# Another order for the first 300 calls of an attention and two-layer kernel on one core

## The chip, the cores and the metric

The kernel runs on one core of one Trainium2 chip. The metric is the device time of one execution in microseconds (us). The core has five engines that run side by side, each through its own list of instructions in order: TensorE (PE in the profile, its weight loads PEld), VectorE (DVE), ScalarE (ACT), GpSimd (POOL) and SyncE (SP), which here only issues transfers. Engines wait for each other by semaphores. Transfers (DMAs) are issued by SP, POOL and, at the end, ACT.

## The reference

Inputs are q, k, v of shape 8 x 12 x 448 x 64 (batch, heads, rows, width), two gains g_q, g_k of 64, and w_in (768 x 2048), w_out (2048 x 768), alpha (2048).

```
q_n = q / sqrt(mean(q*q) + 1e-6) * g_q          # each row of 64; k_n likewise
scores = (q_n @ k_n.T) / 8
attn = exp(scores - max) ; attn = attn / sum(attn)
x = (attn @ v), heads side by side              # 3584 x 768
h = x @ w_in                                    # 3584 x 2048
g = max(h, 0) + alpha * min(h, 0)
out = g @ w_out                                 # 3584 x 768
```

## The kernel before

The 96 heads are cut into 24 groups of four heads, numbered y = 0 to 23. Three groups make one batch b. A group goes through these steps, which the code calls by name with y as the first argument:

- `load_qk` brings q and k into `nat` (SP). There are four `nat` buffers of which a group takes two; the groups 2, 5 and 8 use `arena` instead, so that 5 has to wait until `scale` has read 2, and 4 until `scale` has read 1.
- `square`, `reduce`, `root`, `scale` are the norm: squares (POOL, L376, or ACT, L370), sums of a row (DVE, L395), 1/sqrt as Exp of Ln (ACT, L416 and L417), and the product in fp16 (L436; DVE for groups 1 to 3, POOL from 4 on).
- `turn` (or `turn_one`) transposes q and k by matmuls with an identity into PSUM and copies them out on DVE (L560 to L569, L513 to L523). The product of the two gains goes onto k in that copy.
- `score` (L588) is four small matmuls for one seventh of the keys, `soft` (L602) the exponential of it on ACT, 128x896 elements. A group has seven of each.
- `den` and `attend` (L613) are the sums and the products with v; `log` and `invert` (L666, L671) give the reciprocal of the sums on ACT, `times` (L709) writes the quotient into `xT` on DVE.

When the three groups of a batch are in `xT`, `up(b,ft)` (L726) makes one of 16 blocks of h; `slope` (L766 on ACT, L761 on DVE) writes alpha*h and `larger` (L772) the larger of the two. `begin(ft)` does the first four of six matmuls of `up(0,ft)` before group 2 is there; `up(0,2)` then also ends block 3. `down` and, later, four-product forms make the output.

Group 0 has a form of its own in smaller parts: `part_square`, `part_reduce`, `part_root`, `part_scale`, `part_turn`, `part_copy`. `spin(n)` are idle matmuls on zeros, in fp32 where no second argument is given (two records each) and in fp16 with `spin(n,0)`. `follow(y,nm)` is a POOL copy of one element of the scaled group: POOL waits there until that group is scaled. `gains()` multiplies g_q and g_k after `opening()` has loaded them and alpha into `rows` and has transposed `rows` (the tile `ct`, L1025).

All of it is written down as one list of calls, PLAN, and issued in this order under a manual schedule: each engine meets its instructions in the order of the list, and there is no planner behind it.

Scores have three places in PSUM: two tiles "sc", and one tile "acc", which a score takes with a last argument of 1. `den` and the pair of tiles for `begin(2)` and `begin(3)` take "acc" as well, `attend` takes "acc", "sc" or the two tiles "mm". The tiles "mm" (two) serve `turn`, `spin`, `up` and the other half of `attend`. A new user of a place waits until the last reader of the old one is done.

Of the kernel before, what the change touches and what calls it, by code (L numbers as in the profile page):

```python
# [48 lines left out]
soft(4,0) square(7,q) larger(0,8) up(0,11,0) load_qk(8) score(4,2,0) score(3,3,0) soft(3,5)
load_v(1) square(7,k) up(0,7,1) soft(4,1) slope(0,9) up(0,10,0) reduce(6,q) square(8,q) reduce(6,k)  # L50
load_w_out(2) soft(4,2) up(0,12,0) slope(0,11) larger(0,9) soft(3,3) score(3,4,0) slope(0,10)
score(4,3,0) larger(0,11) larger(0,10) slope(0,7) larger(0,7) up(0,13,0) soft(3,4) slope(0,12)
larger(0,12) turn(5) up(0,14,0) square(8,k) soft(4,3) score(4,6,0) slope(0,13) score(4,4,1) root(6)
slope(0,14) larger(0,13) up(0,15,0) scale(6,q) reduce(8,q) soft(4,4) score(5,4,0) larger(0,14)
scale(6,k) score(5,0,1) reduce(7,q) slope(0,15) larger(0,15) down(1,0,0) score(5,2,1) score(4,5,0)
soft(4,6) soft(5,0) soft(5,4) soft(5,2) score(5,1,0) soft(4,5) down(0,0,0) turn(6) load_w_out(3)
den(3+4,1) reduce(7,k) attend(3+4,0,0) score(5,5,0) score(5,6,0) soft(5,1) mix_weights(0,1) log(3+4)
invert(3+4) soft(5,5) soft(5,6) mix_weights(0,3) attend(3+4,1,0) score(6,0,1) score(5,3,0) soft(6,0)
score(6,4,0) down_end(0,0) down(2,0,0) soft(5,3) root(7) scale(7,q) load_qk(9) soft(6,4) scale(7,k)
den(5,0) attend(5,0,1) down_end(1,0) mix_weights(0,2) times(3+4,0,0) times(3+4,1,0) times(3+4,1,1)  # L60
load_qk(10) log(5) down(0,1,0) reduce(8,k) invert(5) down_end(2,0) times(5,0,1) times(5,0,0)
times(5,0,3) times(5,0,2) score(6,5,1) mix_weights(0,0) score(6,1,0) down_end(0,1) score(6,6,0)
soft(6,5) turn(7) up(1,1,1) square(9,q) down(1,1,0) root(8) reduce(9,q) soft(6,6) score(6,3,1)
score(7,0,0) slope(1,1) score(6,2,0) up(1,2,0) up(1,0,0) soft(6,1) soft(7,0) soft(6,3) square(9,k)
up(1,3,1) up(1,4,0) slope(1,2) slope(1,0) larger(1,1) down_end(1,1) reduce(9,k) root(9) larger(1,2)
# [1032 lines left out]
```

## Time and profile before

| | us |
|---|---|
| three runs | 410.44, 410.85, 411.13; median 410.85 |
| the profiled execution, its own time | 410.69 |
| its span, first to last instruction | 408.6 |
| PE, DVE, ACT, POOL busy | 395.3, 268.3, 270.4, 299.9 |
| first score | 14.24 |
| first `up(0,0)` | 41.30 |
| `attend(6+7,0,0)`, where both lists are the same again | 118.51 |

Times in the profile are counted from the first instruction. A line of the timeline gives start, length, engine, line, operation, tiles and count, and in brackets the idle time of the engine just before it and what ended that. A line with x6 is six instructions in a row whose length is from the start of the first to the end of the last; neighbours overlap a little, so that one exponential of 0.916 us follows the next after some 0.83 us. PE records overlap too: four matmuls of a score alone take 0.38 us from start to end, but two scores in a row 0.57.

### The profile page before, as it was taken

The numbers are of one execution on the slowest core, as the hardware profiler recorded it, in microseconds if no ns is written. First come the engines' busy times: TensorE is split into PE (matmuls) and PEld (weight loads), VectorE is DVE, ScalarE is ACT, GpSimd is POOL, SyncE is SP. The second block draws the span as 40 slices with busy tenths as digits, with TensorE's granted clock in tenths as the row PEclk, the third lists the DMA queues.
The fourth block names the chain that finished last, engine by engine and source line by source line (L and its number), as shares of the span: only waits on it lengthen the run. The fifth ranks groups of instructions, "written<-read, shape, count | busy, mean of one in ns | idle before, by whom it ended". The sixth has DMA issues, their size and how long they took to land.

```text
span 408.6 us, 11992 instructions
## 1 busy us (share of the span) xinstructions
PE 395.3 (97%) x5083; PEld 210.3 (51%) x5083; DVE 268.3 (66%) x480; ACT 270.4 (66%) x405; POOL 299.9 (73%) x200
## 2 busy tenths in 40 slices
PE   7688999999999999999999999999999999999996
PEld 3344445555455445554455455555555455655664
DVE  3957874676766685779678678886668545654422
ACT  5597686757885876767886987686876874245110
POOL 7977998497796998997796995589496809600780
PEclk9999999999999999999999999999999999999999
DMA  7999699796776794579952595794516000230143
GB/s 260 242 280 227 110 265 165 173 239 177 125 180 154 173 203 108 119 172 185 232 130 83 136 240 145 147 217 102 140 38 131 21 2 22 59 79 0 39 98 98
DMA packets 37222, 58.39 MB, mean 143 GB/s; under 512 B 4769, under 2 KB 28977, under 8 KB 37169
## 3 DMA queue, kind: packets, MB, share of 16 engines
q1 hardware_dynamic: 23232, 45.43, 43.2%
q0 software_dynamic: 13536, 11.81, 19.1%
q8 instruction: 39, 0.64, 0.7%
q10 hardware_dynamic: 400, 0.39, 0.3%
q14 instruction: 15, 0.11, 0.1%
HBM read 58.40 MB, written 11.01 MB: 170 GB/s over the span
## 4 chain that ended last, share of the span: by engine, by line
PE 88%; DVE 4%; DMA 3%; POOL 3%; issue 1%; POOLq 0%; DVEq 0%
PE hT L726 25%; PE hTa L726 9%; PE sc L588 8%; PE op L792 7%; PE qx L854 5%; PE av L613 5%; PE qz L854 4%; PE qc L854 4%; PE oq L854 4%; PE qxa L854 3%; PE avb L613 2%; PE dn L613 2%; PE oqm L854 2%; DMA w_in_sb<-in_moe_w_in_dram 2%; POOL nat L376 2%; DMA arena<-in_g_k_dram 2%
## 5 line engine op out<-in xcount | busy, mean ns | idle before, releaser
L602 ACT ACTIVATE expT<-sc 128x896 f16<-128x896 f32 x168 | 146.3, 916 | 40.9 <-PE sc L588 39.2
L726 PE MATMUL hT<-xT,w_in_sb 128*128 128x448 f16 x558 | 115.9, 353 | 1.6 <-DVE xT L709 1.4
L726 PEld LDWEIGHTS <-w_in_sb 128*128 128x128 f16 x768 | 73.0, 98 | 74.5 <-issue 9.9
L423 POOL TENSOR_TENSOR qs<-nat,rr 128x896 f16<-128x896 f32 x30 | 65.7, 2221 | 26.5 <-ACT rr L417 23.4
L766 ACT ACTIVATE gT<-hT,cols 128x448 f16<-128x448 f32 x92 | 58.4, 636 | 40.0 <-PE hT L726 38.9
L772 DVE TENSOR_TENSOR gT<-hT,gT 128x448 f16<-128x448 f32 x93 | 57.3, 619 | 38.2 <-ACT gT L766 37.5
L365 POOL TENSOR_TENSOR nat<-nat 128x896 f32<-128x896 f32 x30 | 50.7, 1697 | 8.1 <-DMA nat<-in_q_dram 7.7
L588 PE MATMUL sc<-qT,kT 64*32 64x448 f16 (+1 forms) x1092 | 49.4, 355 | 4.3 <-ACT expT L602 1.7
L854 PEld LDWEIGHTS <-gT 128*128 128x128 f16 x352 | 33.4, 98 | 25.5 <-issue 4.1
L726 PE MATMUL hTa<-xT,w_in_sb 128*128 128x448 f16 x198 | 42.9, 353 | 0.0
L842 POOL TENSOR_TENSOR gs<-gT 128x1024 f16<-128x1024 f16 x4 | 8.5, 2127 | 36.7 <-DVE gT L772 36.7
L709 DVE TENSOR_TENSOR xT<-av,rden 64x448 f16<-64x448 f32 (+1 forms) x37 | 27.2, 736 | 10.7 <-ACT rden L671 4.6
L386 DVE TENSOR_REDUCE sp<-nat 128x28 f32<-128x896 f32 x30 | 32.1, 1070 | 2.1 <-POOL nat L365 2.0
L588 PEld LDWEIGHTS <-kT 64*32 64x32 f16 (+1 forms) x1092 | 16.7, 93 | 32.4 <-issue 23.0
L792 PE MATMUL op<-w_out_sb,gT 128*128 128x384 f16 x176 | 30.3, 326 | 0.2 <-DVE xT L709 0.2
L766 ACT ACTIVATE gT<-hTa,cols 128x448 f16<-128x448 f32 x33 | 21.0, 636 | 10.5 <-PE hTa L726 10.0
L772 DVE TENSOR_TENSOR gT<-hTa,gT 128x448 f16<-128x448 f32 x33 | 20.4, 618 | 10.6 <-ACT gT L766 10.2
L613 PEld LDWEIGHTS <-vt 64*32 64x32 f16 x1344 | 19.7, 92 | 12.2 <-issue 1.9
L792 PEld LDWEIGHTS <-gT 128*128 128x128 f16 x192 | 18.3, 98 | 14.5 <-issue 3.0
L613 PE MATMUL av<-expT,vt 64*32 64x448 f16 x896 | 24.3, 350 | 0.0
L850 POOL TENSOR_TENSOR gT<-gT 128x1024 f16<-128x1024 f16 x11 | 23.5, 2133 | 0.0
L854 PEld LDWEIGHTS <-arena 128*128 128x128 f16 x136 | 12.6, 98 | 10.5 <-issue 2.3
(151 smaller groups left out, 572.5 us busy)
## 6 DMA issues: line engine op xcount, KB each, us to landing
nat<-in_q_dram SPq DMA_DIRECT2D x60, 216.0 KB, 4.1
nat<-in_k_dram SPq DMA_DIRECT2D x60, 216.0 KB, 5.0
out_dram<-osb SPq DMA_DIRECT2D x107, 96.0 KB, 3.1
vt<-in_v_dram POOLq DMA_DIRECT2D x8, 672.0 KB, 7.8
w_in_sb<-in_moe_w_in_dram POOLq DMA_DIRECT2D x24, 128.0 KB, 7.3
w_out_sb<-in_moe_w_out_dram POOLq DMA_DIRECT2D x4, 768.0 KB, 8.6
nat<-in_k_dram SPq DMA_DIRECT2D x6, 448.0 KB, 7.8
nat<-in_q_dram SPq DMA_DIRECT2D x5, 448.0 KB, 6.7
```

Of the source, the lines that this page charges most:

```text
L365: nc.gpsimd.tensor_mul(out=sqs[y, nm], in0=t[:, :, :HD], in1=t[:, :, :HD])
L386: nc.vector.tensor_reduce(out=parts[y][:, ts("qk".index(nm), 4 * J), :1], in_=sqs[y, nm], axis=AXIS_X, op=ALU.add,)
L423: nc.gpsimd.tensor_mul(out=t.rearrange("p j d n -> p n j d"), in0=nat[y, nm][:, :, :HD].rearrange("p (n j) d -> p n j d", j=J), in1=r.unsq ...
L588: nc.tensor.matmul(out=sc[ds(64 * g + m * c, m), par, :S].rearrange("p (j c) -> p j c", j=J), lhsT=kT[ds(64 * par, 64), j, g, ts(c, m)], r ...
L602: nc.scalar.activation(out=expT[y][:, j], in_=scs[y, j][:, :, :S], func=AF.Exp, scale=QK_SCALE, bias=EXP_BIAS,)
L613: nc.tensor.matmul(out=accs[g][ds(32 * n, 32), :S], lhsT=weights(g, y, par, c, j), rhs=expT[y][ds(64 * g, 64), j, par, :], start=(j == 0), ...
L709: nc.vector.tensor_mul(out=o, in0=p, in1=q)
L726: nc.tensor.matmul(out=hT[:, :S], lhsT=w_in_sb[:, block_of(g, i), ts(ft, 128)], rhs=xT[b][:, g, i, :], start=(i == 0 and g == 0), stop=(i ...
L766: nc.scalar.activation(out=g, in_=hT[:, :S], func=AF.Copy, scale=alpha_sb[:, ft : ft + 1])
L772: nc.vector.tensor_max(out=g, in0=hT[:, :S], in1=g)
L792: nc.tensor.matmul(out=op[:, :OH], lhsT=gT[:, ft, ts(tile % J, 128)], rhs=w_out_sb[:, ft, ts(oh, OH)], start=(ft == 0), stop=(ft == NF - 1),)
L854: nc.tensor.matmul(out=bank[:, c], lhsT=g[:, ft], rhs=v[:, ft, c], start=(first and ft == 0), stop=(ft == HF - 1), skip_group_check=True,)
```

## The change

The list of calls up to `fold(11)` is put in another order, and from there on it is the same. What changes with it:

- ScalarE takes the squares of 1k, 2q, 4q, 6q, 6k and 8k from GpSimd (1q was there already), and the copies out of PSUM of group 0's q and of a part of its k from VectorE. VectorE takes the slopes of blocks 6, 8, 9, 13, 14, 15 of batch 0 and 4 and 5 of batch 1; block 12 goes to ScalarE, 2 stays on VectorE and 3 goes to ScalarE.
- `rows` is filled by two gain transfers ahead of alpha, where it was alpha and four gain transfers. The transpose of `rows` is a call of its own, `factors()`, behind the transposes of q.
- v is loaded ahead of the first w_in piece; w_in comes in six pieces, 1 and 0 (rows below 512), 0 (rows above), 2 (above), 2 and 3 (below). Group 5 is loaded ahead of group 4.
- Idle matmuls: before, 2 in fp32 and 19 in fp16, then 4 in fp32 and 1 in fp16 before and between scores. After, 22 in fp16 and 2 in fp32 ahead of the transposes of q, 15 in fp16 from there to the first score, and 15 in fp16 and 2 in fp32 between later scores.
- 34 calls of `follow` stand where there were 4.

```diff
 PLAN = """
-opening() part_square(q,0:1,0:7,act) part_square(q,1:2,0:7,act) part_reduce(q,0:1,0:7) spin(2,0)
-part_reduce(q,1:2,0:7) part_root(q,0:7) part_square(k,0:2,0:3,act) part_scale(q,0:7,7,pool)
-part_reduce(k,0:2,0:3) part_square(k,0:2,3:7,act) square(1,q) load_w_in(1) spin(1)
-part_reduce(k,0:2,3:7) part_root(k,3:7) reduce(1,q) square(1,k) part_root(k,0:3) gains()
-part_turn(q,r0-7) load_qk(3) spin(1,0) part_scale(k,0:3,3,vec) part_turn(k,r0-3)
-part_scale(k,3:7,4,vec) part_copy(q,0:7,vec) part_turn(k,r3-7) load_v(0) reduce(1,k) follow(0,k)
-square(2,q) part_copy(k,0:3,vec) part_copy(k,3:7,vec) root(1) square(2,k) score(0,0,0) soft(0,0)
-reduce(2,q,0) score(0,4,1) load_w_in(0) score(0,3,0) spin(1) reduce(2,q,1) soft(0,3) score(0,1,0)
-scale(1,k) scale(1,q) soft(0,4) score(0,2,0) soft(0,2) reduce(2,k) score(0,6,1) turn_one(1,q)
-soft(0,1) turn_one(1,k) score(1,0,1) score(1,3,0) spin(1) score(1,2,0) soft(0,6) root(2) soft(1,0)
...
-log(0+1) load_qk(5) score(2,1,0) spin(1) reduce(3,k,0+1) attend(0+1,1,0) score(2,6,0) score(2,4,1)
-attend(0+1,0,1) soft(2,1) root(3) score(2,3,1) invert(0+1) scale(3,q) scale(3,k) score(2,2,0)
-load_w_in(3) soft(2,4) soft(2,6) times(0+1,1,0) times(0+1,1,1) square(4,q) times(0+1,0,0) turn(3)
-score(2,5,0) square(4,k) load_qk(6) reduce(4,q,None) soft(2,3) soft(2,2) soft(2,5) den(2,0) log(2)
-reduce(4,k,None) invert(2) attend(2,0,1) score(3,0,1) square(5,q) square(5,k) times(2,0,0)
-score(3,1,0) begin(0) reduce(5,q) square(6,q) soft(3,0) begin(1) up(0,0,0) load_w_out(0) reduce(5,k)
-up(0,1,0) begin(2) begin(3) root(4) up(0,2,0) up(0,3,1) up(0,4,0) scale(4,q) slope(0,0) soft(3,1)
...
+opening() spin(1,0) spin(1,0) part_square(q,1:2,0:7,act) part_reduce(q,1:2,0:7)
+part_square(q,0:1,0:7,act) spin(18,0) part_reduce(q,0:1,0:7) part_root(q,0:7)
+part_scale(q,0:7,7,pool) part_square(k,0:2,0:3,act) spin(1,0) spin(1,0) part_square(k,0:2,3:7,act)
+spin(2) part_reduce(k,0:2,0:3) part_reduce(k,0:2,3:7) part_root(k,0:7) part_scale(k,3:7,4,vec)
+part_turn(q,r0-7) spin(2,0) factors() spin(1,0) part_scale(k,0:3,3,vec) spin(3,0) part_turn(k,r0-3)
+load_v(0) spin(3,0) part_copy(q,0:7,act) spin(2,0) gains() square(1,k,act) square(1,q,act) spin(1,0)
+spin(3,0) reduce(1,k) part_copy(k,0:3,act) square(2,q,act,2) load_w_in(1,0,4) square(2,k)
+reduce(1,q) score(0,0,1) root(1) part_turn(k,r3-7) load_w_in(0,0,4) part_copy(k,3:7,vec) load_qk(3)
+score(0,4,0) reduce(2,q,1) score(0,3,0) spin(1,0) scale(1,k) soft(0,0) spin(1,0) scale(1,q)
+reduce(2,k) score(0,6,1) spin(1,0) spin(5,0) score(0,1,0) follow(1,q) score(0,2,0) load_w_in(0,4,8)
+soft(0,3) soft(0,4) square(3,k) soft(0,6) soft(0,1) turn_one(1,q) turn_one(1,k) reduce(2,q,0)
+root(2) score(1,0,1) load_w_in(2,4,8) soft(0,2) spin(1,0) score(1,3,0) spin(1,0) score(0,5,1)
+soft(1,0) score(1,2,0) square(3,q) soft(1,3) spin(1,0) soft(1,2) scale(2,k) spin(1,0) spin(1)
+follow(2,k) score(1,1,0) follow(1,q) scale(2,q) follow(2,k) soft(0,5) score(1,5,0) turn(2) soft(1,1)
+follow(2,q) follow(2,k) score(1,6,1) reduce(3,k,0+1) spin(1) soft(1,5) spin(1,0) score(1,4,0)
+soft(1,6) score(2,0,0) load_qk(5) load_w_in(2,0,4) soft(1,4) den(0+1,0) score(2,1,0) load_qk(4)
+soft(2,0) square(4,k) spin(2,0) load_w_in(3,0,4) attend(0+1,0,1) reduce(3,q,None) square(5,q)
+log(0+1) score(2,4,1) soft(2,1) score(2,6,0) root(3) invert(0+1) attend(0+1,1,1) scale(3,q)
+times(0+1,1,1) score(2,3,0) scale(3,k) soft(2,6) score(2,2,1) times(0+1,1,0) soft(2,4) follow(2,q)
+turn(3) soft(2,3) soft(2,2) score(2,5,0) soft(2,5) follow(2,k) den(2,0) log(2) attend(2,0,1)
+square(5,k) score(3,0,1) square(4,q,act) times(0+1,0,0) reduce(4,q,None) invert(2) times(2,0,0)
+score(3,1,0) begin(0) follow(2,k) reduce(4,k,None) begin(1) begin(2) up(0,0,0) load_qk(6) begin(3)
+soft(3,0) square(6,q,act) up(0,3,0) load_w_out(0) slope(0,0) reduce(5,q) up(0,1,0) root(4) up(0,2,0)
+slope(0,1) follow(2,k) larger(0,0) follow(3,k) reduce(5,k) soft(3,1) up(0,4,0) scale(4,q)
+larger(0,1) slope(0,3) score(3,2,0) follow(2,k) load_qk(7) slope(0,2,vec) scale(4,k) score(3,5,0)
+slope(0,4) larger(0,4) up(0,5,0) up(0,6,0) soft(3,2) slope(0,5) larger(0,2) follow(1,k) larger(0,3)
+larger(0,5) slope(0,6,vec) root(5) soft(3,5) load_w_out(1) follow(2,k) turn(4) score(3,6,0)
...
-    def load_w_in(c):
+    def load_w_in(c, lo, hi):
...
+        for m in range(lo, hi):
+            e, n = divmod(m % 4, 2)
...
-    def square(y, nm):
+    def square(y, nm, eng=None, n=1):
...
+            if eng is nc.scalar:
+                nc.scalar.activation(out=sqf[:, c], in_=src[:, c], func=AF.Square)
+            else:
...
-        if nm == "k":
+        if nm == "k" and eng is nc.scalar:
+            nc.scalar.activation(out=o, in_=tp, func=AF.Copy, scale=gain[:, 0:1])
+        elif nm == "k":
...
-    def slope(b, ft):
+    def slope(b, ft, eng=None):
         hT, g = raised[b, ft]
-        if b == 0 and ft in (2, 3, NF - 4):
+        if eng is nc.vector:
...
     def opening():
         load_qk(0)
         nc.scalar.preload_act_table_set("natural_log_exp_and_others")
+        for n, g in enumerate((g_q, g_k)):
+            nc.gpsimd.dma_start(
+                out=rows[NF + n : NF + n + 1].rearrange("o (h d) -> o h d", h=2),
+                in_=g.unsqueeze(0).unsqueeze(0).broadcast_to((1, 2, D)),
+            )
         nc.gpsimd.dma_start(out=rows[:NF], in_=moe_alpha.rearrange("(t p) -> t p", p=128))
-        for n, g in enumerate((g_q, g_k)):
-            for h in range(2):
-                nc.gpsimd.dma_start(
-                    out=rows[NF + n : NF + n + 1, ds(64 * h, 64)], in_=g.unsqueeze(0)
-                )
         load_qk(1, True)
         load_qk(2)
 
-        spin(2)
-        spin(17, False)
-        ct = psf.tile([128, 512], FP32, name="ct", tag="mm")
+    def factors():
+        ct = pss.tile([128, 2, 512], FP32, name="ct", tag="sc")[:, 0]
         nc.tensor.transpose(ct[:, : NF + 2], rows, ident32[: NF + 2, : NF + 2])
         held_ct.append(ct)
 
     def gains():
         nc.vector.tensor_copy(out=cols, in_=held_ct[0][:, : NF + 2])
-        nc.vector.tensor_mul(
-            out=gain, in0=cols[:, NF : NF + 1], in1=cols[:, NF + 1 : NF + 2]
+        nc.vector.tensor_scalar(
+            out=gain, in0=held_ct[0][:, NF : NF + 1], scalar1=cols[:, NF + 1 : NF + 2],
+            scalar2=None, op0=ALU.mult,
         )
```

More of the change, by code (lines that the diff above doesn't have):

```diff
@@ L49 @@
[L49 to L65, printed above, removed]
@@ new lines @@
+score(4,4,0) scale(6,q) soft(4,4) larger(0,13) slope(0,14,vec) score(4,6,0) score(5,0,1)
+larger(0,14) up(0,15,0) slope(0,15,vec) scale(6,k) score(5,4,0) larger(0,15) soft(5,0) down(1,0,0)
+soft(4,6) reduce(8,k) reduce(7,q) square(7,k) score(4,5,0) follow(5,q) score(5,2,1) score(5,1,0)
+down_end(1,0) soft(5,4) soft(4,5) down(0,0,0) soft(5,2) turn(6) den(3+4,1) soft(5,1) load_w_out(3)
+log(3+4) invert(3+4) score(5,6,1) attend(3+4,0,1) soft(5,6) attend(3+4,1,0) score(6,0,1)
+score(5,3,0) soft(6,0) score(5,5,0) mix_weights(0,1) reduce(7,k) soft(5,3) down_end(0,0) soft(5,5)
@@ new lines @@
+load_qk(9) down(2,0,0) down(0,1,0) score(6,4,0) times(3+4,0,0) den(5,1) times(3+4,1,0) log(5)
+root(7) attend(5,0,1) soft(6,4) scale(7,q) invert(5) score(6,5,1) times(3+4,1,1) score(6,1,0)
+times(5,0,0) times(5,0,1) down_end(2,0) load_qk(10) mix_weights(0,3) follow(1,k) follow(1,k)
+times(5,0,3) down_end(0,1) soft(6,5) times(5,0,2) square(9,q) scale(7,k) score(6,6,0) turn(7)
+reduce(8,q) mix_weights(0,2) up(1,1,1) slope(1,1) reduce(9,q) down(1,1,0) larger(1,1)
+mix_weights(0,0) soft(6,6) soft(6,1) score(7,0,0) score(6,3,1) up(1,2,0) up(1,0,0) up(1,3,1) root(8)
@@ new lines @@
+flip(9,k) weigh(9) score(8,1,0) down(3,0,0) scale(10,q) square(11,k) down_end(2,1) score(8,2,0)
+scale(10,k) flip(9,q) soft(8,5) reduce(11,k) reduce(11,q) soft(8,4) soft(8,1) score(8,6,0) fold(11)
+load_qk(13) attend(6+7,0,0) attend(6+7,1,0) score(9,1,0) score(9,0,0) down_end(3,0) soft(8,2)
+invert(6+7) score(9,2,1) down(3,1,0) times(6+7,0,0) soft(8,6) root(11) times(6+7,1,0) load_qk(14)
+flip(10,q) down(4,0,1) mix_weights(1,2) soft(9,0) times(6+7,1,1) score(9,5,0) square(12,q) soft(9,1)
+soft(9,2) scale(11,q) score(9,3,0) square(12,k) reduce(12,q) down_end(3,1) soft(9,5)
@@ new lines @@
+fold(13) den(9+10,1) slope(2,11) mix_weights(3,3) qa1(6,0) up(2,15,0) qa2(6,1) root(13)
+mix_weights(3,0) flip(12,q) slope(2,9) larger(2,14) larger(2,13) down(5,0,0) log(9+10) slope(2,15)
+larger(2,11) larger(2,9) invert(9+10) soft(11,0) square(14,k) flip(12,k) reduce(14,q) weigh(12)
+qa1v(6) larger(2,15) mix_weights(2,1) scale(13,q) score(11,3,1) scale(13,k) score(11,4,0)
+attend(9+10,0,1) mix_two(6,pool) soft(11,4) qa2v(6) mix_rest(6) score(11,1,0) down_end(5,0)
+times(9+10,0,0) soft(11,3) square(15,q) reduce(14,k) attend(9+10,1,0) score(12,0,0) soft(11,1)
```

111 lines of the change are left out of this document (48 added, 63 removed).

## The prediction

> **What bounds the kernel now.** I read the page's shares first, then the chain of waits, then the timelines of the first 50 us.
>
> ```profile
> PE 395.3 (97%) x5083; PEld 210.3 (51%) x5083; DVE 268.3 (66%) x480; ACT 270.4 (66%) x405; POOL 299.9 (73%) x200
> PE 88%; DVE 4%; DMA 3%; POOL 3%; issue 1%; POOLq 0%; DVEq 0%
> ```
>
> TensorE carries 88% of the chain. The chain in order of time says where it does not:
>
> ```profile
> 3.82 6.24 DMA arena<-in_g_k_dram
> 10.06 0.14 issue
> 10.20 0.22 PE ct L1025
> ...
> 22.48 3.46 POOL nat L376 x3
> 25.94 0.54 POOL w_in_sb L339
> 26.48 7.31 DMA w_in_sb<-in_moe_w_in_dram
> ...
> 35.80 3.34 POOL nat L376 x2
> ...
> 40.16 1.09 DVE xT L709
> 41.25 0.04 issue
> 41.30 0.92 PE hT L726 x4
> ```
>
> Up to 41.30 other engines set the pace: a gain transfer that holds the first transposes until 10.06, then squares and w_in transfers on GpSimd. From 41.30 TensorE is without a break to speak of (20.48 of 20.7 us busy to 62.0), so whatever the first 41 us lose or win reaches the end of the kernel, and nothing can be won later. What the chain hides is ScalarE, hardly less late:
>
> ```profile
> 13.90 0.23 ACT L416 ACTIVATE rr<-ss 128x28 f32<-128x28 f32 x1 [3.94 <-DVE ss L395]
> 14.68 4.97 ACT L602 ACTIVATE expT<-sc 128x896 f16<-128x896 f32 x6 [0.30 <-PE sc L588]
> 20.24 7.50 ACT L602 ACTIVATE expT<-sc 128x896 f16<-128x896 f32 x9 [0.23 <-PE sc L588]
> 35.08 0.92 ACT L602 ACTIVATE expT<-sc 128x896 f16<-128x896 f32 x1 [0.48 <-PE sc L588]
> 36.74 0.92 ACT L666 ACTIVATE rden<-dn 128x896 f32<-128x896 f32 x1 [0.74 <-PE dn L613]
> 37.69 0.95 ACT L671 ACTIVATE rden<-rden 128x896 f32<-128x896 f32 x1
> ```
>
> It is busy 20.06 of the 21.4 us from the first exponential to the 21st, which ends at 36.0. `invert(2)` ends at 38.64; `times(2,0,0)` could follow but stands behind `reduce(4,k)` on VectorE, which waits for a GpSimd square until 39.13. So the two paths are 1.5 us apart, and a change that frees GpSimd gains 1.5 us at most before ScalarE binds.
>
> **The change part by part.** I follow the new order through the engines with the durations of the old rows, against the profiled execution (410.69; the median of the runs, 410.85, is 0.16 above it, and I put the difference onto the median).
>
> *Idle matmuls ahead of the transposes of q.* TensorE now has 22 in fp16 and 2 in fp32 there, and nothing else to wait for.
>
> ```profile
> 4.62 4.50 PE L1000 MATMUL spin<-gT,ident 128*128 128x448 f16 x17
> 6.49 0.15 PEld L1000 LDWEIGHTS <-ident 128*128 128x128 f16 x1 [0.22 <-issue]
> 6.86 1.82 PEld L1000 LDWEIGHTS <-ident 128*128 128x128 f16 x10 [0.22 <-issue]
> ```
>
> Until 6.86 they start 0.37 apart, then ten take 1.82 (0.187 each): TensorE doubles its speed there. An fp32 one took 1.57 before that (two from 1.47 to 4.62) and 0.80 after it (10.72 to 11.52). With the same moment, (6.86 - 1.47)/0.373 = 14.4 are done by 6.86, the other 7.6 take 1.41, two in fp32 1.6: TensorE is free at 9.87. Bounds: 7.2 if all run fast, 12.8 if all run slow. I take 9.87, since TensorE starts work at the same 1.47. [...]
>
> *Gains.* Two gain transfers and alpha are all issued by 3.35 (rows 0.49 and 0.70); those of before landed 3.9 to 6.3 after issue, so `rows` is there by 9.7, ahead of `factors()` at 10.6. The old wait to 10.06 is gone, but nothing is gained: TensorE is behind its own idle matmuls until 9.87. The new form of the gain product is bounded by 0.04 and 0.62 (rows of L1030) and has 1.5 us of cover.
>
> *ScalarE before the first exponential.* The root of k is done at 8.9, and ScalarE then stands at `part_copy(q)`, in order, until the transposes (0.45) end: 10.4. Behind it: the copy of q (between 0.61, the VectorE copy, and 0.92, an exponential of the same size; next to another one 0.83, which I take: same engine), squares of 1k and 1q at 0.86 (8.32 to 9.18), the copy of a part of k (0.40 to 0.55; 0.40), two halves of 2q (1.10 for two, 1.0 in a row): 14.35. `root(1)` 0.50: first exponential at 14.85 against 14.68, **+0.17**. VectorE's sums of 1k and 1q (1.0 each) end at 14.2, the first score at 13.9; both are covered. VectorE loses 1.1 us of copies that were on its path, but ScalarE now sets the start.
>
> *`root(2)`.* It stands after the fifth exponential and needs `reduce(2,q,0)`, which VectorE has behind the copies of `turn_one`. Their transposes are behind `score(0,2)` on TensorE, which needs the place that the third exponential frees, 2.6 after the first: 17.4. Then a score and 14 transposes (0.2 + 0.95) to 18.6, copies to 19.65 (0.61 and 0.79 before), the half sum 0.53, the root 0.5: the next exponential starts at 20.75, while five would have ended at 19.0. The seventh starts at 21.58 against 20.24: **+1.34**. In the order before, both halves of the sum come ahead of `scale(1)`, and the root costs no wait.
>
> *To `log(2)`.* An fp32 idle matmul after `score(1,6)` needs a tile "mm", so it waits for a copy of `turn(2)`, and `score(1,4)` behind it is 0.25 late. `attend(0+1,1,1)` comes after the other half, so `times(0+1,1,1)` waits for it until 33.3 (avb was done at 30.5 before); `turn(3)` and `score(2,5)` follow. But the same stretch had 0.88 us of waits before. The last exponential starts at 36.55 against 35.08, `log(2)` at 38.15 against 36.74: **+1.41**.
>
> *Group 4 and the first blocks.* The square of 4q stands between `log(2)` and `invert(2)`: 0.86. `invert(2)` ends at 40.8, `reduce(4,q)` at 41.0, `times(2,0,0)` at 42.1 (before 41.25); `reduce(4,k)` now comes behind it. `begin(2)` stands ahead of `up(0,0)` and needs the tile that `soft(3,0)` frees at 41.6, so TensorE has `up(0,0)` at 42.4. It then has one block of `begin` less to do: `up(0,4)` starts 2.28 (12 matmuls) later, at 44.7, against 44.32: **+0.4**. The freed GpSimd is worth its 1.0 here (1.41 down to 0.4), and no more.
>
> *Behind 44.7.* VectorE has six more slopes and two fewer on batch 0: 4 x 0.6 on 16.29 of 20.7 us, near nine tenths. ScalarE gives slopes of 0.64 and takes squares of 0.95, about even. GpSimd loses three squares of 1.67 there and gets 30 more `follow` at 0.19, 5.7 us, half of them here; they read what GpSimd or VectorE made long before. On SP group 4 now stands behind group 5, whose load waits for `scale(2)` to about 23; group 4 is asked for at 23.7 and 24.1 where it was 17.03 and 18.03. Transfers asked for at 22 to 23 took 8.7 and 11.3, and now four share that spot: 4k lands between 33 and 37. GpSimd waits for it at `square(4,k)`, with the last w_in piece and the squares of 5 queued behind; `scale(4,k)` is then done between 47.4 and 48.9, and `turn(4)` wants it at 48.8. Bounds 0 and 2.0 (nothing of it can gain, TensorE being full); I take **+0.5**, as the slack lies within the landing's spread. v ahead of w_in costs nothing: v was needed at 28.9, w_in piece 1 at 44.
>
> Sum: 0.4 + 0.5 = +0.9, 411.59 on the profiled execution's scale, **411.75** on the median's.
>
> **The rivals.** A: *faster.* ScalarE is not late at `log(2)`. The chain, which names GpSimd and the w_in transfers for 22 to 39, speaks for it; 20.06 busy of 21.4 on ScalarE speaks against it. The place is `root(2)`: if its sum comes in time, the lag is about 0.2 instead of 1.41, and with nothing lost later the kernel takes 410.85 - 0.8 to 410.85 - 1.0, 409.9 to 410.0. It decides for faster below a lag of 0.2, since `up(0,4)` moves by the lag less 1.0. An earlier full speed of TensorE adds up to 0.75.
>
> B: *no change to speak of.* The full speed comes at 5.0: TensorE is free at 8.9, everything on ScalarE moves by 0.75 (its root of k, 8.9, allows no more than 1.45), the lag is 0.65, `up(0,4)` is 0.35 early, and the 0.5 behind it makes 411.0. For it: the moment is one record of one execution. Against: 6.86 is the only row.
>
> C: *slower by two and more.* GpSimd gets 4k at 37 and `turn(4)` waits, or VectorE at nine tenths holds the tiles of `up`: 0.4 + 2.0 gives 413.25. For it: GpSimd was 20.50 of 20.7 us busy there. Against: it loses three squares.
>
> **How the numbers follow.** The forecast has 0.31, C 0.19, B 0.28, A 0.22. A difference of less than 0.2%, 0.8 us, could not be told from none. A is faster, B the same, the forecast and C slower: 0.22, 0.28, 0.50. The forecast's own range is 411.1 to 412.5. For 8 in 10 it reaches to 409.7, A with some of the earlier clock, and to 413.3, C.
>
> **What would show it.** In the changed profile: ScalarE idle from 8.9 to about 10.4 and ended by the transposes (L485); the first exponential near 14.9; about 1.2 us of ScalarE idle ahead of L416 near 20, ended by VectorE's sum; `up(0,0)` near 42.4 with three begun blocks ahead of it; `square(4,k)` on GpSimd idle for a transfer of k until 33 or later; TensorE full from then on. The prediction is wrong if the transposes of q start before 9, if `root(2)` finds its sum waiting, or if TensorE stands for the tiles of VectorE between 45 and 62.

## The result, and the profile after

The changed kernel takes 433.56 us (median of 4, 432.52 to 434.75) where the kernel before takes 410.99 (410.44 to 412.18): a ratio of 1.0546, 95% interval 1.0503 to 1.0589. I had forecast 411.75. Ratios here and below leave disturbed executions out, so that one can differ a little from the quotient of two medians.

The profiled execution of after took 434.51 (span 432.7). The busy times and the chain of its page, against 97% and 88% for PE before:

```profile
PE 405.2 (94%) x5111; PEld 213.8 (49%) x5111; DVE 272.1 (63%) x484; ACT 272.5 (63%) x406; POOL 294.1 (68%) x220
PE 80%; POOL 7%; DMA 4%; issue 4%; DVE 2%; ACT 2%; SPq 1%; POOLq 0%; DVEq 0%; ACTq 0%
```

TensorE has lost share, and most of what it waits for lies behind the opening. (A stand, below, is a stretch in which TensorE waits.) I cut the trace at the starts of the sums `den`, which every kernel here has in the same order:

| us | start of den(0+1) | to den(3+4) | to den(6+7) | to den(9+10) | from there to the end |
|---|---|---|---|---|---|
| before | 26.16 | 44.55 | 39.68 | 44.35 | 253.86 |
| after | 27.65 | 54.90 | 48.45 | 46.61 | 255.09 |
| more | 1.49 | 10.35 | 8.77 | 2.26 | 1.23 |

*The opening* of this profile comes near what I had worked out. ScalarE after:

```profile
13.66 0.92 ACT L610 ACTIVATE expT<-sc 128x896 f16<-128x896 f32 x1
...
20.20 0.23 ACT L422 ACTIVATE rr<-ss 128x28 f32<-128x28 f32 x1 [1.64 <-DVE ss L401]
...
38.42 0.92 ACT L674 ACTIVATE rden<-dn 128x896 f32<-128x896 f32 x1 [0.74 <-PE dn L621]
```

Its first exponential is at 13.66 (before 14.68), then it waits 1.64 us at `root(2)` for VectorE's sum, and `log(2)` is 1.7 late.

*The first stand, 10.4.* The timeline of ScalarE, SP and TensorE after; a line has start, length, what ran, and in brackets the idle time before it and what ended that:

```profile
55.11 0.64 SPq L314 DMA_DIRECT2D arena<-in_k_dram  x1
...
65.31 0.95 ACT L380 ACTIVATE arena<-arena 128x896 f32<-128x896 f32 x1 [9.17 <-DMA arena<-in_k_dram]
...
67.12 0.59 PE L596 MATMUL sc<-qT,kT 64*64 64x448 f16 x4 [7.57 <-ACT expT L610]
...
68.30 2.40 PE L734 MATMUL hT<-xT,w_in_sb 128*128 128x448 f16 x6 [0.60 <-DVE gT L780]
```

`square(8,k,act)` stands on ScalarE ahead of `soft(3,3)`. Its k is asked for at 55.11, since `arena` is free no sooner than after `scale(5,k)`, and lands 10.1 later. ScalarE waits 9.17 us in order, the exponentials behind it wait with it, and TensorE waits 7.57 for a place for its scores. In the kernel before the same square stands on GpSimd, which comes to it just as its k lands, 6.6 after it was asked for:

```profile
54.33 0.37 SPq L306 DMA_DIRECT2D arena<-in_k_dram  x1
...
61.11 1.68 POOL L376 TENSOR_TENSOR arena<-arena 128x896 f32<-128x896 f32 x1
```

So 3.5 of the wait are the longer transfer, 10.1 for 6.6. From the asking to the start of the square that waits for this one transfer it is 6.4 us in e12 (56.45 to 62.86), 6.5 in e8 (53.54 to 60.00), 8.7 in e13 (57.58 to 66.28) and 10.2 in after (55.11 to 65.31); what makes it long was not tried.

Behind the stand TensorE runs slowly: six matmuls of `up` take 2.40 where they take 1.30, at a granted clock of 0.50 from 65 to 70. The table by stretches (PE, PEld, DVE, ACT, POOL busy with counts; then granted clock, DMA share, GB/s):

```profile
60.00:65.00 5.00, 0.00 (x0) 0.00 (x0) 0.00 (x0) 0.00 (x0) 1.80 (x2) 0.71 1.23 241
65.00:70.00 5.00, 2.28 (x9) 0.95 (x9) 1.78 (x3) 4.65 (x9) 1.43 (x1) 0.50 0.84 131
70.00:75.00 5.00, 5.00 (x39) 2.97 (x38) 3.42 (x6) 1.77 (x3) 4.98 (x6) 0.76 0.02 4
```

*The second, 8.8.* `root(7)` stands behind `log(5)`, which needs `den(5)`, which TensorE now has behind two `down` instead of one. The first three lines are of before, where `root(7)` comes ahead of `log(5)`, the others of after:

```profile
77.63 0.23 ACT L416 ACTIVATE rr<-ss 128x28 f32<-128x28 f32 x1
78.19 3.34 POOL L436 TENSOR_TENSOR qs<-nat,rr 128x896 f16<-128x896 f32 x2 [6.04 <-ACT rr L417]
80.02 0.54 ACT L666 ACTIVATE rden<-dn 128x448 f32<-128x448 f32 x1 [1.10 <-PE dn L637]
...
94.48 0.54 ACT L674 ACTIVATE rden<-dn 128x448 f32<-128x448 f32 x1 [4.43 <-issue]
...
95.08 1.52 PE L621 MATMUL av<-expT,vt 64*32 64x448 f16 x56 [0.71 <-ACT rden L674]
...
95.53 1.69 POOL L442 TENSOR_TENSOR qs<-nat,rr 128x896 f16<-128x896 f32 x1 [19.31 <-ACT rr L423]
...
100.37 0.59 PE L596 MATMUL sc<-qT,kT 64*64 64x448 f16 x4 [3.27 <-DVE xT L717]
...
102.59 0.93 PE L568 MATMUL tps<-ident,qs 128*128 128x128 f16 x7 [0.77 <-POOL qs L442]
```

GpSimd idles 19.31 us for a root whose sums were there at 84.9, and TensorE stands for the quotient of group 5 and for group 7.

*The third, 2.3.* The square of 11q waits for its transfer, which was asked for at 121.27, and its k is asked for 9.8 later (before 4.3, at 95.82 and 100.09):

```profile
121.27 1.73 SPq L329 DMA_DIRECT2D nat<-in_q_dram  x4
...
127.20 1.68 POOL L373 TENSOR_TENSOR nat<-nat 128x896 f32<-128x896 f32 x1 [4.50 <-DMA nat<-in_q_dram]
```

### The profile page after: what moved, and what is told of

Read it like the earlier page. It is cut to its first block, busy times and chain, and to the rows that moved or that the text cites. A ratio compares the mean times of both kernels' runs of the same rounds, so it can differ in the third digit from the quotient of the medians.

```text
span 432.7 us, 12070 instructions
## 1 busy us (share of the span) xinstructions
PE 405.2 (94%) x5111; PEld 213.8 (49%) x5111; DVE 272.1 (63%) x484; ACT 272.5 (63%) x406; POOL 294.1 (68%) x220
## 4 chain that ended last, share of the span: by engine, by line
PE 80%; POOL 7%; DMA 4%; issue 4%; DVE 2%; ACT 2%; SPq 1%; POOLq 0%; DVEq 0%; ACTq 0%
PE hT L734 21%; PE hTa L734 7%; PE sc L596 7%; PE qx L862 5%; PE av L621 4%; PE op L800 4%; PE qc L862 4%; PE qz L862 4%; PE spin L1008 4%; PE oq L862 3%; PE dn L621 3%; PE avb L621 3%; PE qxa L862 3%; DMA arena<-in_k_dram 2%; POOL qs L442 2%
## 5 line engine op out<-in xcount | busy, mean ns | idle before, releaser
L734 PE MATMUL hT<-xT,w_in_sb 128*128 128x448 f16 x558 | 117.3, 356 | 0.8 <-DVE gT L780 0.6
L734 PEld LDWEIGHTS <-w_in_sb 128*128 128x128 f16 x768 | 73.7, 99 | 75.1 <-issue 11.8
L429 POOL TENSOR_TENSOR qs<-nat,rr 128x896 f16<-128x896 f32 x30 | 65.7, 2220 | 20.5 <-ACT rr L423 20.2
L774 ACT ACTIVATE gT<-hT,cols 128x448 f16<-128x448 f32 x86 | 54.5, 634 | 36.5 <-PE hT L734 35.5
L596 PE MATMUL sc<-qT,kT 64*32 64x448 f16 (+1 forms) x1092 | 50.6, 357 | 14.2 <-ACT expT L610 9.4
L734 PE MATMUL hTa<-xT,w_in_sb 128*128 128x448 f16 x198 | 44.0, 359 | 0.0
L442 POOL TENSOR_TENSOR qs<-nat,rr 128x896 f16<-128x896 f32 x6 | 10.1, 1686 | 23.0 <-ACT rr L423 23.0
```

Of the source, the lines that this page charges most:

```text
L429: nc.gpsimd.tensor_mul(out=t.rearrange("p j d n -> p n j d"), in0=nat[y, nm][:, :, :HD].rearrange("p (n j) d -> p n j d", j=J), in1=r.unsq ...
L596: nc.tensor.matmul(out=sc[ds(64 * g + m * c, m), par, :S].rearrange("p (j c) -> p j c", j=J), lhsT=kT[ds(64 * par, 64), j, g, ts(c, m)], r ...
L734: nc.tensor.matmul(out=hT[:, :S], lhsT=w_in_sb[:, block_of(g, i), ts(ft, 128)], rhs=xT[b][:, g, i, :], start=(i == 0 and g == 0), stop=(i ...
L774: nc.scalar.activation(out=g, in_=hT[:, :S], func=AF.Copy, scale=alpha_sb[:, ft : ft + 1])
```

## The experiments

Beside each run the kernel before was timed on the same chip; its median there stands in the headings. "The first part" is the list through `up(0,4,0)`, "the rest" what stands behind it.

### Which part loses (before: 411.95; for e8 411.83)

e1 has the first part of after and the rest of before; e8 has the first part of before and the rest of after.

> The changed kernel's order through up(0,4,0) (the first 44 us), and from there on the order of the kernel before. Theory 1 (all but 0.9 us of the loss is made by the order behind up(0,4), which began 45.22 against 44.32): 411.9, between 411.3 and 412.8. Rival (the first part leaves group 4, the transfers or the queues in a state from which the rest is late whatever its order): 418 or more.

> The other half of e1: the order of the kernel before through up(0,4,0), and the changed kernel's order behind it. Theory 1 (the first stand ends when the k of 8 lands, at 65.3 in the changed kernel and 66.4 in e3 though its opening was 4 us later there, so that the opening's lateness is swallowed by it): nearly all of the loss is here, 430.5 to 433.5, and e1's 5 and this loss add up to more than the whole change's 22. Rival (the parts add): 411.4 + 22.6 - 5 = 429 or less.

e1: 416.90, ratio 1.0124 (1.0094 to 1.0154). e8: 432.79, ratio 1.0479 (1.0428 to 1.0530). My 411.9 for e1 is missed by 5: the first part alone loses 5, not 0.9. e8's loss is 21, and 5 and 21 are more than the 22.6 of the whole, as I had forecast. But in e8 the k of 8 landed at 59.9, earlier than the 65.3 I had named, TensorE stood 3.55 for it, and the third stretch took 49.45 (5.1 more than before, against 2.3 in after), so the excess of the sum is not one stand's doing.

### Three causes in the rest (before: 411.95, from e9 on 412.11)

e2 moves one call, e3 three, e4 both; e9 adds a `down`, e10 the two products of group 9.

```diff
 e2, e4   -larger(0,9) square(8,k,act) soft(3,3)
          +larger(0,9) soft(3,3)
          -soft(4,6) reduce(8,k)
          +soft(4,6) square(8,k,act) reduce(8,k)
 e3, e4   -soft(5,5) load_qk(9)
          +soft(5,5) root(7) scale(7,q) scale(7,k) load_qk(9)
          -log(5) root(7) attend(5,0,1) soft(6,4) scale(7,q) invert(5)
          +log(5) attend(5,0,1) soft(6,4) invert(5)
          -square(9,q) scale(7,k) score(6,6,0)
          +square(9,q) score(6,6,0)
 e9       -down(2,0,0) down(0,1,0) score(6,4,0)
          +down(2,0,0) score(6,4,0)
          -attend(5,0,1) soft(6,4)
          +attend(5,0,1) down(0,1,0) soft(6,4)
 e10      -scale(8,k) up(1,5,1)
          +scale(8,k) scale(9,q) up(1,5,1)
          -mix_weights(1,1) slope(1,5,vec)
          +mix_weights(1,1) scale(9,k) slope(1,5,vec)
          -soft(7,2) scale(9,q) score(7,3,0)
          +soft(7,2) score(7,3,0)
          -den(6+7,1) scale(9,k) larger(1,12)
          +den(6+7,1) larger(1,12)
```

> The changed kernel with one call moved: square(8,k,act), still on ScalarE, stands behind soft(4,6) instead of ahead of soft(3,3). Theory 1 (three stands of TensorE with a cause each; the first is ScalarE waiting in order for the k of 8 at this square, and is 10.9 of the 11.83 us by which down(1,0) is late): 433.6 - 10.9 = 422.7, between 421 and 425. Rival A (the later stands are the first one's consequence): 412 to 414. Rival B (the late transfer holds the kernel from wherever it is waited for): 431 to 434.

> The changed kernel with root(7), scale(7,q) and scale(7,k) moved up from behind log(5) to behind down_end(0,0), that is behind reduce(7,k) and ahead of both downs and den(5). Theory 1 (the second stand comes from root(7) waiting in ScalarE's order for log(5), and that for den(5) behind two downs on TensorE): den(6+7) was 20.6 late after 11.7 at den(5), so 433.6 - 8.9 = 424.7, between 423 and 427. Rival A (the second stand is only the first one's consequence): 433. Rival B (the downs ahead of den(5) hold the quotient of group 5 too, whatever root(7) does): 430 to 433.

> The changed kernel with both moves of the two runs before: square(8,k,act) behind soft(4,6), and root(7) with both products behind down_end(0,0). Theory 1 (separate stands, whose prices add): 433.6 - 10.9 - 8.9 = 413.8, between 412.5 and 416, of which 0.9 is from the first 44 us and 2.3 a third stand near 125 to 150 us that stays. Rival (the prices don't add, since one stand hides part of the other): 418 to 424, or 411 if the third stand was a consequence of the two.

> The kernel of e4 (425.0) with one more call moved: down(0,1,0) stands behind attend(5,0,1) instead of ahead of den(5,1). In e4 TensorE stood 0.67 us ahead of attend(5) and 3.27 us behind it, the second for VectorE's quotients of group 5, with no other work left in its list. Theory 1 (both downs ahead of den(5) leave nothing to cover the quotient of group 5): 425.0 - 3.5 = 421.5, between 420.5 and 422.5. Rival (VectorE's own order, the copies of the downs' results between the quotients, holds TensorE all the same): 424 to 425.

> The kernel of e9 with scale(9,q) moved to right behind scale(8,k) and scale(9,k) to right behind mix_weights(1,1), that is ahead of square(11,q) on GpSimd. In e4 group 11's q was asked for at 111.43 and its k at 121.36, each behind the product that frees its place, and the second product stood on GpSimd behind the square of the first (landed 117.48). Theory 1 (this is the third stand: TensorE stood 1.03 and 2.58 us there, and the stretch took 48.57 instead of 44.35): 4.2 less than e9, about 417.3, between 416 and 418.5, which is e1's 416.9. Rival (the loads are late for another reason and the stand stays): 421 or more.

| | us | ratio, interval | den(0+1) | to den(3+4) | to den(6+7) | to den(9+10) |
|---|---|---|---|---|---|---|
| e2, 8k later | 429.05 | 1.0432 (1.0396 to 1.0467) | 31.30 | 43.45 | 48.09 | 48.66 |
| e3, root(7) early | 432.81 | 1.0511 (1.0476 to 1.0546) | 31.90 | 50.89 | 45.45 | 47.20 |
| e4, both | 425.00 | 1.0317 (1.0283 to 1.0350) | 31.35 | 43.44 | 45.88 | 48.57 |
| e9, and down(0,1) | 422.15 | 1.0245 (1.0218 to 1.0271) | 30.30 | 43.44 | 44.07 | 48.70 |
| e10, and scale(9) | 419.38 | 1.0149 (1.0097 to 1.0200) | 27.65 | 43.48 | 43.71 | 44.35 |

The totals of e2 to e4 are missed by 6 to 11, the stretches show why. In e2 the first stand is gone to the full (43.45 for 54.90), so that square's place is its cause. But the kernel wins 4.5 only, since its opening is 3.65 later than in the profile of after and nothing swallows that any more, and its third stretch is 2.05 longer. In e3 the root's place is worth 3.0 of the 8.8, not all of it: TensorE stood on, for the quotient, with both `down` already spent. The timeline of TensorE in e4:

```profile
87.62 1.52 PE L620 MATMUL av<-expT,vt 64*32 64x448 f16 x56 [0.67 <-ACT rden L673]
...
92.92 0.38 PE L595 MATMUL sc<-qT,kT 64*64 64x448 f16 x4 [3.27 <-DVE xT L716]
```

e9 puts `down(0,1)` into that gap and the wait is 0.67 instead of 3.27; the kernel wins 2.85, inside the range forecast, and the stretch gives 1.8 of it. e10 takes the third stretch to 44.35, that of before to the last digit, 4.35 less than in e9. The kernel wins 2.8 by its median, where I had 4.2, and 419.38 lies above the 418.5 that I had named; the profiled execution, 415.96, is the fastest of its four. In e4 group 11's q and k had been asked for at 111.43 and 121.36, 10 apart, since the product that frees k's place stood behind a square that waited for q:

```profile
111.43 1.73 SPq L328 DMA_DIRECT2D nat<-in_q_dram  x4
...
121.36 1.72 SPq L328 DMA_DIRECT2D nat<-in_k_dram  x4
```

What stays in e10's middle stretch is 4.0. TensorE's waits there are 0.67 (log of 5), 0.67 (quotient), 1.04 (product of 8) and 1.03 (exponential ahead of `den(6+7)`), 3.4 in sum; I did not take these apart.

Is the square's place enough by itself? e12 is the kernel before with that one call moved:

```diff
-larger(0,9) soft(3,3)
+larger(0,9) square(8,k,act) soft(3,3)
-up(0,14,0) square(8,k) soft(4,3)
+up(0,14,0) soft(4,3)
```

> The kernel before with one call moved: the square of 8k on ScalarE, ahead of soft(3,3), instead of on GpSimd behind up(0,14,0). The k of 8 was asked for at 54.33 and landed 6.6 later, 60.9, in the kernel before; ScalarE reaches the place at 58.0. Theory 1 (the price is what the transfer is late at that place, and it is paid by TensorE): 3.0 of wait and 0.9 of square, some 3 of it on TensorE: 411.8 + 3 = 414.8, between 413.5 and 417. Rival A (a square on ScalarE costs at most its own 0.95): 411.8 to 412.8. Rival B (the place alone costs what it cost in the changed kernel): 421 or more.

418.26 (before 412.11), ratio 1.0155 (1.0119 to 1.0191): 6 us for one call, twice what I had worked out. The wait is longer, since this execution asked for k at 56.45 and not 54.33, and the clock falls behind it, to 0.50 from 65 to 70 (ScalarE and TensorE of e12):

```profile
62.86 0.95 ACT L370 ACTIVATE arena<-arena 128x896 f32<-128x896 f32 x1 [5.19 <-DMA arena<-in_k_dram]
...
64.67 0.59 PE L588 MATMUL sc<-qT,kT 64*64 64x448 f16 x4 [4.48 <-ACT expT L602]
...
65.86 2.40 PE L726 MATMUL hT<-xT,w_in_sb 128*128 128x448 f16 x6 [0.60 <-DVE gT L772]
```

The stretch to `den(3+4)` took 52.83, 8.3 more, of which 4.5 is the stand: I had left the half clock out of the price.

### The opening (before: 411.90 for e13 to e15, 411.83 for e5 to e7)

e13 is the changed kernel again.

> The changed kernel once more, unchanged, for a second profile of its opening. Theory 1 (its opening differs from execution to execution with the moment of full speed on TensorE and with a half clock behind the stand at root(2), and the first stand, which ends with the transfer of the k of 8, swallows that): den(0+1) anywhere from 27.6 to 32, den(3+4) at 82.5 to 83 all the same, 432.5 to 434.5 in all. Rival (its opening is always the one of the first profile, 27.65, and the other kernels' 30 to 32 has another cause): 27.65 again.

434.25, ratio 1.0547 (1.0498 to 1.0597). The same program has another opening: `den(0+1)` at 31.71 instead of 27.65, `up(0,4)` at 48.95 instead of 45.22, and `den(3+4)` at 82.97 instead of 82.55. The first stand swallowed 3.6 of 4.1: TensorE stood 5.42 there and not 7.57, and full speed was back at most 4.5 us behind its end (from 68.09 to six matmuls of `up` in 1.30 at 72.55) and not 5.3 (from 67.12 to the clock's rise at 72.38). Of the eight profiles with this opening (after, e1 to e4, e9, e10, e13) two have `den(0+1)` at 27.65 and six at 30.30 to 31.90, so the first profile was a lucky one. TensorE's timeline in e13, and the table by stretches of it:

```profile
23.88 0.60 PE L596 MATMUL sc<-qT,kT 64*64 64x448 f16 x8 [1.88 <-ACT expT L610]
24.42 0.93 PE L1008 MATMUL spin<-gT,ident 128*128 128x448 f16 x2
25.14 1.75 PE L1008 MATMUL spin<-gT 128*128 128x448 f32 x2
...
28.79 0.95 PE L568 MATMUL tps<-ident,qs 128*128 128x128 f16 x14 [1.00 <-DVE qs L442]
```

```profile
20.00:24.00 4.00, 1.53 (x17) 0.64 (x18) 3.39 (x5) 2.33 (x6) 3.79 (x6) 1.00 1.15 159
24.00:28.00 4.00, 3.79 (x20) 0.85 (x15) 4.00 (x2) 2.79 (x4) 3.98 (x6) 0.57 0.82 121
28.00:32.00 4.00, 3.20 (x45) 1.67 (x53) 3.34 (x6) 2.47 (x4) 3.71 (x9) 1.00 0.87 197
```

Both profiles have the same stand of 1.88 behind `root(2)`; only here half speed follows it (two fp32 idle matmuls 1.75 instead of 1.02). Full speed came at 4.04 in the first profile (where the weight loads of the idle matmuls begin to follow each other without 0.22 between them) and at 7.03 in this one, at 5.84 in e2 and 7.02 in e1. So two profiles of one program differ by 3.0 in it, and 4.04 is only 2.6 behind TensorE's start at 1.47.

The last matmul line waits for VectorE, whose products of group 2 are long. The same two in e13 and in e6 (least, median, most in ns; first and last start):

```profile
L442 DVE TENSOR_TENSOR qs<-arena,rr x2: 2661/3278/3894, 22.3 to 24.8; 128x896 f16<-128x896 f32 x2
```

```profile
L438 DVE TENSOR_TENSOR qs<-arena,rr x2: 1084/1088/1093, 21.9 to 22.9; 128x896 f16<-128x896 f32 x2
```

e5, e6 and e7 are e1 with one or both of these moves; e14 is e6 with idle matmuls in the stand; e15 is e7 with fewer ahead of the transposes of q:

```diff
 e5, e7, e15   -scale(1,q) reduce(2,k)
               +scale(1,q) reduce(2,q,0) reduce(2,k)
               -turn_one(1,k) reduce(2,q,0) root(2)
               +turn_one(1,k) root(2)
 e6, e7, e14,  -soft(0,4) square(3,k) soft(0,6)
 e15           +soft(0,4) soft(0,6)
               -score(1,2,0) square(3,q) soft(1,3)
               +score(1,2,0) soft(1,3)
               -soft(1,1) follow(2,q) follow(2,k)
               +soft(1,1) follow(2,q) square(3,k) square(3,q) follow(2,k)
 e14           -spin(1,0) score(0,5,1)
               +spin(1,0) spin(9,0) score(0,5,1)
 e15           -spin(18,0)
               +spin(10,0)
```

> The kernel of e1 (new order through up(0,4,0), old order behind it: 416.9) with one call moved: reduce(2,q,0) stands ahead of reduce(2,k) on VectorE instead of behind the copies of turn_one(1,q) and turn_one(1,k). In e1 ScalarE stood 1.64 us at root(2), TensorE 1.88 us for the exponential behind it, then ran at a granted clock of 0.57 from 24 to 28. Theory 1 (this wait is what costs in the opening, with the half clock that follows): 416.9 - 1.6 - 1.6 = 413.7, and down to 412 if VectorE's product behind it is early too. Rival (the two products of group 2 on VectorE, 2.64 and 3.89 us in e1 and 1.08 each in the kernel before, hold turn(2) until 28.7 whatever ScalarE does): 415.5 to 417.

> The kernel of e1 (416.9) with two calls moved: square(3,k) and square(3,q) on GpSimd stand behind the first follow(2,q), that is behind both products of group 2 on VectorE, where the order before has them. Theory 1 (VectorE's products of group 2 are long because GpSimd works beside them): the products fall from 2.64 and 3.89 to 1.08 each, turn(2) waits no more (0.95), and the kernel is at 416.9 - 1.0 = 415.9, with the half clock of 24 to 28 left. Rival A (the products are long for another reason, the transfers): products unchanged, 416.9. Rival B (the squares, now some 2 us later, are missed by root(3)): 417.5 or more.

> The kernel of e1 (416.9) with both moves of the two runs before: reduce(2,q,0) ahead of reduce(2,k), and square(3,k) and square(3,q) behind the first follow(2,q). Theory 1 (the wait of root(2), the half clock behind it and GpSimd beside VectorE's products make up the loss of the opening): 416.9 - 1.6 - 1.6 - 1.0 = 412.7, and between 410.5 and 413, since ScalarE's first exponential is there 0.2 to 1.0 earlier than before. Rival (something else in the opening, the later moment of full speed on TensorE or the transfers): 414 or more.

> The kernel of e6 (the new order through up(0,4,0), the old one behind it, squares of 3 held back: 416.4) with nine more fp16 idle matmuls (some 0.19 each, 1.7 us) ahead of score(0,5,1), where TensorE stands 1.88 us for the exponential behind root(2). The root's wait stays. Theory 1 (the half clock behind the stand is most of what the opening loses; of e6's executions the one at a mean clock of 1.000 took 412.66, those at 0.992 to 0.996 took 415 to 418.8): 412.5 to 413.8. Rival (the wait of ScalarE itself is the loss): 415.5 to 416.5.

> The kernel of e7 (413.6) with 14 instead of 22 fp16 idle matmuls ahead of the transposes of q. In e7 ScalarE waited 1.46 us for these transposes, TensorE being behind its idle matmuls until 9.42. Theory 1 (they hold the start): ScalarE's copy of q at 8.6 to 9.2 instead of 10.0, first exponential 0.8 to 1.4 earlier than 14.53, 412.2 to 412.8. Rival (with fewer of them full speed comes later, or VectorE's sums of 1q and 1k hold the first exponential): 413.3 to 414.5.

| | us | ratio, interval | den(0+1) |
|---|---|---|---|
| e5, sum of 2q earlier | 413.35 | 1.0029 (1.0006 to 1.0051) | 27.43 |
| e6, squares of 3 held back | 416.44 | 1.0097 (1.0062 to 1.0131) | 30.29 |
| e7, both | 413.57 | 1.0048 (1.0018 to 1.0078) | 27.00 |
| e14, e6 with idle matmuls | 417.55 | 1.0138 (1.0087 to 1.0190) | 29.07 |
| e15, e7 with fewer ahead | 412.15 | 1.0013 (0.9982 to 1.0044) | 25.98 |

e5 shows the largest part of the opening's loss: one reduction, moved ahead, gives back 3.5 of e1's 5. ScalarE's root follows its fifth exponential with no wait (1.64 in e1 and after):

```profile
16.51 3.35 ACT L606 ACTIVATE expT<-sc 128x896 f16<-128x896 f32 x4 [0.64 <-PE sc L592]
19.91 0.23 ACT L418 ACTIVATE rr<-ss 128x28 f32<-128x28 f32 x1
```

With it TensorE's 1.88 is gone, the clock is 1.00 throughout, and VectorE's products are 1.08 each again. e6 shows whose doing their length was: with the squares behind them they take 1.08 to 1.09. In e13 a square ran on GpSimd from 22.26 to 23.95 and one from 26.08 to 27.77; the two products ended 0.96 behind each (22.25 + 2.66 = 24.91; 22.25 + 6.48 = 28.73). So each product ended behind a square. The rows leave open why the second product, which started 1.24 ahead of its square and takes 1.08 alone, did not end before it. The kernel before keeps the squares away with `follow(2,q)`. But in time e6 wins nothing that can be told from e1, 0.5, since TensorE stands (1.88) and slows there (0.63 from 24 to 28) all the same; of e6's executions one had a mean clock of 1.000 and took 412.66, those at 0.991 to 0.996 took 414.97 to 418.81. e7, with both moves, is no faster than e5 and lies 0.6 above the range that I had named.

e14 was to show the clock's share and does not. The filled stand keeps 24 to 28 at 1.00 and `den(0+1)` comes 1.2 earlier than in e6, but the kernel is no faster, and its one execution at a mean clock of 1.000 still took 415.31. Its profile has another stand, in the middle of a product with v, that no semaphore ends:

```profile
33.40 1.51 PE L618 MATMUL avb<-expT,vt 64*32 64x448 f16 x55
37.16 0.36 PE L618 MATMUL avb<-expT,vt 64*32 64x448 f16 x1 [2.24 <-issue]
```

The clock is 0.72 and 0.50 behind it (36 to 40, 40 to 44). e15 starts its first exponential at 13.51 against 14.53 in e7 and wins 1.4; it ends even with before.

### The whole, and the moves alone (before: 412.11 for e11, 411.90 for e16)

e11 is the changed kernel with the moves of e10 and e7, so that all engines keep the work that the change gave them. e16 is the order of before with four things of the change alone, two gain transfers, the later transpose of `rows`, and the copy of q and the square of 1k on ScalarE:

```diff
-part_root(k,3:7) reduce(1,q) square(1,k) part_root(k,0:3) gains()
-part_turn(q,r0-7) load_qk(3)
+part_root(k,3:7) reduce(1,q) part_root(k,0:3)
+part_turn(q,r0-7) factors() gains() load_qk(3)
...
-part_copy(q,0:7,vec)
+part_copy(q,0:7,act) square(1,k,act)
```

> The changed kernel with all places found so far put back: square(8,k,act) later, root(7) with both products earlier, down(0,1,0) later, both products of 9 earlier, reduce(2,q,0) earlier, squares of 3 behind the first follow(2,q). All engines keep the work that the change gave them. Theory 1 (these places are the whole loss): e10 less the 3.4 of e5 and e7, about 413.9, between 412 and 415. Rival (the other division of the work between the engines has a price of its own): 416 or more.

> The order of the kernel before throughout, with four things of the change alone: two gain transfers ahead of alpha, the transpose of rows behind those of q, and on ScalarE the copy of q out of PSUM and the square of 1k. Theory 1 (ScalarE stood 3.94 us ahead of its first exponential in the kernel before, and VectorE and GpSimd were full; what is moved there is free): the first exponential 0.5 to 1.0 earlier than 14.68, GpSimd 1.7 us ahead, 411.0 to 411.6, below the 411.8 of the kernel before. Rival A (ScalarE from the first exponential on binds and something later than up(0,4) takes it back): 411.8 to 412.3. Rival B (the chain through the square of 1k on ScalarE is longer): 412.5 or more.

e11: 416.71, ratio 1.0102 (1.0069 to 1.0135), above the 412 to 415 that I had named and in the range of the rival. So 18 of the 22.6 us are found and some 4.6 are not, and whether the other division of the work costs them is not shown. Of these the 4.0 of the middle stretch (45.15 there, with 1.52 of a stand like e14's) is the larger part. e16: 411.31, ratio 0.9989 (0.9963 to 1.0014). Its first exponential is at 13.79 against 14.68, as I had it, and the time is not to be told from before. No version tried beats the kernel before.

## Why the prediction was wrong, point by point

- *Idle matmuls ahead of the transposes of q.* Held, in its bounds: TensorE was free at 8.56 and 10.09 in the two profiles, I took 9.87 of 7.2 to 12.8. Transposes of q ahead of 9 were one of my signs of being wrong, and the first profile has them there. That the moment differs from execution to execution (4.04 and 7.03 in the two profiles) I treated as an unknown of one number, not as a spread. The 5.0 of rival B, from which the 0.75 in A and B follows, was an estimate of mine that no run shows: the profiles have 4.04, 5.84, 7.02 and 7.03, and with full speed at 4.04 the first exponential came 1.19 ahead of my 14.85.
- *Gains, and ScalarE before the first exponential.* Held: 13.66 and 15.20 around my 14.85.
- *`root(2)`.* Held in mechanism and near in size: the profile has 1.64 of idle time ended by VectorE's sum, I had about 1.2 (19.0 to 20.75, less the root itself). What the wait does to the clock (0.57 from 24 to 28 in e13) was missing: I costed a stand of TensorE at its length alone. So was GpSimd beside VectorE's products (2.66 and 3.89 in e13, 1.08 and 1.09 in e6): I counted what `follow` costs GpSimd and not what its place keeps apart.
- *To `log(2)`, group 4, first blocks.* `up(0,4)` at 45.22 in the first profile against my 44.7 and before's 44.32, but 48.95 in the second. The first part loses 5 (e1), and 0.9 was the lucky execution; so the +0.4 of the sum is too small by 4 to 5 as well.
- *Behind 44.7: +0.5, bounds 0 to 2.0.* This is the step that failed; it was 21 in e8. "ScalarE gives slopes of 0.64 and takes squares of 0.95, about even" weighs busy time. I followed 4k into its transfer but not 8k, whose square moves to an engine with exponentials queued behind it, and whose transfer cannot be asked for before `scale(5,k)` is done, 54.33 in the profile of before, landing 6.6 later. GpSimd could wait there: its next work was not due. ScalarE could not. For excluding more than 2.0 I gave no reason but the wait at `turn(4)`; that TensorE is full, which I gave for the lower bound, says nothing about losses: it was full because nobody was late.
- *The order behind it.* I did not walk the list to `fold(11)` at all: `root(7)` behind `log(5)`, both `down` ahead of `den(5)`, `scale(9,k)` behind `square(11,q)`. By the stretches, e3, e9 and e10 price the places at 3.0, 1.8 and 4.4.
- *The rivals.* C had the right side and a wrong place (4k, VectorE), at a tenth of the size. What it asks for came true, k of 4 landed at 37.6, 11.8 after it was asked for, but `turn(4)` waited no more than 0.40 for it. A and B fall.

The moves onto ScalarE themselves are about even in time for the two of them that e16 has; for all of them e11 leaves 4.6 us that may be theirs.

## What to carry to other kernels

When an operation moves to another engine, price what it waits for, at its new place in that engine's order, and who is queued behind it: a 0.95 us square cost its stretch 10 us here (the whole kernel 4.5 by e2, 7.8 by e4 against e3), and 6 by itself in the old kernel. A late stand in a list written by hand can hide an earlier loss, so one stretch's price is read from the trace by marks that all kernels share, and a fix that wins less than its stretch shows has uncovered something. And a stand of TensorE is to be costed at more than its length, because the clock may fall behind it: in e12 the stand took 4.48, and the clock was 0.50 from 65 to 70.

## What was not expected of the hardware

Stands of TensorE of 1.2 to 2.2 us in the middle of a group of equal matmuls, ended by nothing that the profile shows, are there in e5 (1.34), e11 (1.16 and 1.52), e14 (2.24) and e15 (1.90), in places that differ; the profiles of before and after have none of that length. After has two shorter ones: 0.26 until 39.87, 1.45 us after a 16 KB transfer of the instruction queue had ended (38.42), and 0.62 until 285.70, 1.35 after another had (284.35). Around three of the longer ones there is such a transfer too, one each from 75 to 79 in e11, 34 to 38 in e14 and 73 to 77 in e15. Behind most such transfers TensorE does not stand: before has 39 of them from 14 us on and no stand that nothing ends. Whether TensorE waits for instructions there no run tried.

Half speed came back behind every stand over 3.5 us (7.57 in after, 5.42 in e13, 4.48 in e12, 3.55 in e8; six matmuls of `up` took 2.40 behind each, for 1.30), behind the one of 3.27 in after and e13 (six of `up` 2.44) and not in e4 (1.30), and behind the one of 1.88 in seven of the nine profiles that have it, not in after and e10. In after the granted clock falls at 62.14, rises at 72.38, falls at 99.69 and rises at 106.52: half speed lasted 10.2 and 6.8 us. So the length of a stand alone does not decide it; what else does these runs do not show. The table by stretches for the stand of 3.27, two lines of after and two of e4; the columns are those of the table above:

```profile
90.00:100.00 10.00, 6.38 (x145) 3.48 (x142) 3.19 (x6) 3.13 (x7) 4.39 (x5) 0.98 0.70 154
100.00:110.00 10.00, 8.86 (x53) 4.58 (x54) 5.40 (x8) 3.43 (x7) 8.93 (x7) 0.67 0.92 212
...
90.00:100.00 10.00, 7.08 (x57) 4.01 (x58) 8.61 (x15) 4.72 (x9) 7.00 (x7) 1.00 0.74 174
100.00:110.00 10.00, 9.62 (x71) 4.81 (x69) 7.64 (x14) 6.28 (x12) 9.13 (x13) 1.00 0.72 133
```
